# Gate and value products of two token blocks by seven half products instead of eight

## The chip, the cores and the metric

One core of one Trainium2 chip runs the whole program. The metric is device time in microseconds (us). The kernel before took 1024.76 us in the median of three runs (1024.1 to 1025.03). The execution that the profiler recorded took 1026.81 us, of which its trace covers a span of 1025.0 us. Engines are named as in the profile: PE (TensorE), PEld (its weight loads), DVE (VectorE), ACT (ScalarE), POOL (GpSimd), SP (the queue that issues all DMAs here).

## What is computed

A linear attention (random features) is followed by two feed-forward layers on 2304 tokens of 512 features. The change touches the last layer alone:

```python
def _moe2_ref(x, w_gate, w_val, w_out, rms_g):      # x 2304x512, w_gate, w_val 512x1536, w_out 1536x512
    rms = np.sqrt(np.mean(x * x, axis=-1, keepdims=True) + 1e-06)
    xn = x / rms * rms_g
    g = xn @ w_gate
    silu = g * (1.0 / (1.0 + np.exp(-g)))
    val = xn @ w_val
    return (silu * val @ w_out).astype(np.float32)
```

## The kernel before

Tokens are cut into four blocks of 512 columns and a remainder of 256 (`BLK`, index `REM`). The program has two overlapping phases: attention with the first feed-forward layer (`attention`, `moe1`), and then the second layer (`normed`, `moe2`), block by block.

Nothing is ordered by hand. Each piece of work is a node of a `Plan` with an engine (sometimes a choice of engines), an assumed duration, a priority (a position on a common axis; `E1` is the start of the second layer) and buffers out of named pools of slots. `Plan.run` plays the engines forward with these durations, gives each free engine the ready node of the lowest priority whose slots are free, and emits the instructions in that order. On the chip each engine then works through its own list in that fixed order and waits on semaphores. DMAs all go through SP's list.

Every matmul operand is float32 and is cut by `split` into a high part (a CAST on ACT) and a low part (a subtraction, `less`, L389, on DVE or POOL). A product of two such operands takes three matmul passes: high x high, high x low, low x high.

For the second layer, `normed(j)` loads block j's features (`y_d`, four chunks of 128), sums their squares, takes root and reciprocal, scales the chunks, and splits them. `moe2(j)` runs over 12 chunks c of 128 hidden units. `gv(c)` makes gate and value (L991): 4 chunks of features x 3 passes = 12 matmuls each, into a PSUM bank of class `h` (gate) and one of class `t` (value). Silu on ACT (L1002), the product with the value on DVE (L1004) and a split give the operand of `opart(c)` (L1016): for each of 4 groups of 128 tokens 3 matmuls that accumulate over all c in a bank of class `acc`. PSUM has 8 banks: 2 `t`, 2 `h`, 4 `acc`. The weights' 36 units (gate, value and out for each c) are read as 64-bit words, decoded to float32 (`decode`) and split once (`w2_unit`); both parts then stay in SBUF (`wa`, `wb`, some `x`).

## Time and profile before

| | |
|---|---|
| median of 3 runs | 1024.76 us (1024.1 to 1025.03) |
| the profiled execution | 1026.81 us |
| its span in the trace | 1025.0 us |
| PE busy / PEld busy | 1015.3 us (99%) / 864.3 us (84%) |
| DVE / ACT / POOL busy | 519.9 / 470.6 / 85.4 us |
| DMA | 136.86 MB, mean 134 GB/s |
| TensorE clock granted | full speed (2.4 GHz) in every slice |

Busy time of PE counts a matmul from its start to its modelled end; as matmuls overlap, what a matmul costs in a dense row is the distance from start to start, and that is read from the timeline. The second layer starts at 573.5 us and its last matmul ends shortly before 1020 us.

### The profile page before, as it was taken

The numbers are of one execution on the slowest core, as the hardware profiler recorded it, in microseconds if no ns is written. First come the engines' busy times: TensorE is split into PE (matmuls) and PEld (weight loads), VectorE is DVE, ScalarE is ACT, GpSimd is POOL, SyncE is SP. The second block draws the span as 40 slices with busy tenths as digits, with TensorE's granted clock in tenths as the row PEclk, the third lists the DMA queues.
The fourth block names the chain that finished last, engine by engine and source line by source line (L and its number), as shares of the span: only waits on it lengthen the run. The fifth ranks groups of instructions, "written<-read, shape, count | busy, mean of one in ns | idle before, by whom it ended". The sixth has DMA issues, their size and how long they took to land.

```text
span 1025.0 us, 14010 instructions
## 1 busy us (share of the span) xinstructions
PE 1015.3 (99%) x5284; PEld 864.3 (84%) x5284; DVE 519.9 (51%) x1060; ACT 470.6 (46%) x992; POOL 85.4 (8%) x70
## 2 busy tenths in 40 slices
PE   8999999999999999999999999999999999999997
PEld 7888888888888888888889988888888888888897
DVE  5989997744434443278612698822422241213211
ACT  5887897643445434446535566522312231213211
POOL 0111222210101100011100011300000000000000
PEclk9999999999999999999999999999999999999999
DMA  8777888833346322387668343321002100100100
GB/s 250 257 236 255 271 285 299 276 105 110 113 119 196 103 94 83 110 302 263 208 220 273 104 165 124 122 72 42 11 1 73 42 11 1 61 21 1 40 3 21
DMA packets 50644, 136.86 MB, mean 134 GB/s; under 512 B 6160, under 2 KB 7824, under 8 KB 50576
## 3 DMA queue, kind: packets, MB, share of 16 engines
q1 hardware_dynamic: 50576, 135.95, 40.8%
q8 instruction: 42, 0.69, 0.3%
q14 instruction: 26, 0.21, 0.1%
HBM read 114.96 MB, written 20.97 MB: 133 GB/s over the span
## 4 chain that ended last, share of the span: by engine, by line
PE 96%; DMA 2%; ACT 1%; DVE 0%; SPq 0%; issue 0%; ACTq 0%
PE h L840 19%; PE acc L870 19%; PE h L991 14%; PE t L991 14%; PE acc L1016 14%; PE t L726 3%; PE t L599 3%; PE t L596 2%; PE t L666 2%; PE t L721 1%; DMA f<-y 1%; PE acc L596 1%; PE t L768 1%; PE t L669 1%; PE t L730 1%; DMA lt<-in_k_t_dram 0%
## 5 line engine op out<-in xcount | busy, mean ns | idle before, releaser
L389 DVE TENSOR_TENSOR g<-f,g 128x512 fp32r<-128x512 f32 (+1 forms) x135 | 95.8, 709 | 133.6 <-ACT f L510 72.0
L870 PE MATMUL acc<-g,wr 128*128 128x512 f32 (+1 forms) x660 | 151.0, 373 | 0.0
L840 PE MATMUL h<-x,wr 128*128 128x512 f32 x528 | 133.5, 396 | 0.0
L870 PEld LDWEIGHTS acc<-g,wr 128*128 128x128 f32 x660 | 113.7, 189 | 20.0 <-DVE g L389 0.2
L1004 DVE TENSOR_TENSOR f<-t,f 128x512 f32<-128x512 f32 (+1 forms) x58 | 37.1, 640 | 181.7 <-PE t L991 180.9
L840 PEld LDWEIGHTS h<-x,wr 128*128 128x128 f32 x528 | 97.2, 188 | 19.6
L398 ACT CAST g<-f 128x512 fp32r<-128x512 f32 (+1 forms) x60 | 34.9, 582 | 133.9 <-DVE f L1004 87.7
L1002 ACT ACTIVATE f<-h 128x512 f32<-128x512 f32 (+1 forms) x58 | 32.5, 560 | 132.7 <-PE h L991 132.6
L991 PE MATMUL h<-x,wb 128*128 128x512 f32 (+1 forms) x420 | 92.0, 368 | 0.0
L991 PE MATMUL t<-x,wb 128*128 128x512 f32 (+1 forms) x420 | 91.9, 368 | 0.0
L854 ACT ACTIVATE f<-h 128x512 f32<-128x512 f32 (+1 forms) x80 | 44.8, 560 | 102.0 <-PE h L840 95.1
L1016 PE MATMUL acc<-wb,g 128*128 128x512 f32 x378 | 91.6, 389 | 0.0
L991 PEld LDWEIGHTS h<-x,wb 128*128 128x128 f32 x420 | 74.0, 188 | 13.7
L991 PEld LDWEIGHTS t<-x,wb 128*128 128x128 f32 x420 | 73.6, 189 | 13.1
L1016 PEld LDWEIGHTS acc<-wb,g 128*128 128x128 f32 x378 | 70.5, 188 | 14.3
L870 PE MATMUL acc<-g,wu 128*128 128x512 f32 (+1 forms) x300 | 69.6, 375 | 1.2 <-DVE g L389 1.0
L623 ACT ACTIVATE p<-t,sm 128x128 f32<-128x128 f32 x216 | 59.8, 382 | 21.8 <-DVE sm L614 21.8
L991 PE MATMUL h<-x,wa 128*128 128x512 f32 (+1 forms) x300 | 65.8, 368 | 0.0
L991 PE MATMUL t<-x,wa 128*128 128x512 f32 (+1 forms) x300 | 65.7, 368 | 0.0
L840 PE MATMUL h<-x,wu 128*128 128x512 f32 x240 | 61.7, 398 | 0.0
L991 PEld LDWEIGHTS h<-x,wa 128*128 128x128 f32 x300 | 52.8, 188 | 9.7
L991 PEld LDWEIGHTS t<-x,wa 128*128 128x128 f32 x300 | 52.6, 189 | 9.4
(189 smaller groups left out, 1524.4 us busy)
## 6 DMA issues: line engine op xcount, KB each, us to landing
wr<-w1d SPq DMA_DIRECT2D x88, 512.0 KB, 3.5
st<-in_w_out_dram SPq DMA_DIRECT2D x28, 512.0 KB, 4.1
w1d<-wr SPq DMA_DIRECT2D x22, 512.0 KB, 4.1
st<-in_w_in_dram SPq DMA_DIRECT2D x16, 512.0 KB, 4.8
st<-in_w_gate_dram SPq DMA_DIRECT2D x12, 512.0 KB, 4.2
st<-in_w_val_dram SPq DMA_DIRECT2D x12, 512.0 KB, 4.1
f<-y SPq DMA_DIRECT2D x20, 256.0 KB, 4.2
v<-in_v_r_dram SPq DMA_DIRECT2D x16, 260.0 KB, 3.1
```

The source lines that it names most:

```text
L389: return lambda: en.tensor_tensor(out=lo(), in0=src(), in1=f32(hi()), op=ALU.subtract)
L398: first = plan.add("ACT", act(n), prio, lambda: nc.scalar.copy(out=hi(), in_=src()), rd, [whi], after, pre=[blo] if blo is not bhi else [])
L596: nc.tensor.matmul(o, lhsT=xs[0].ap[:, c], rhs=flat(bd), start=True, stop=True)
L599: nc.tensor.matmul(o, lhsT=xs[x].ap[:, cidx, :], rhs=flat(w), start=n == 0, stop=n == 2)
L623: nc.scalar.activation(out=pbuf.ap[:, j0 + i, :], in_=fp.ap[:, i, :], func=AF.Exp, bias=mx.ap[:, i:i + 1])
L840: nc.tensor.matmul(hb.ap[:, :n], lhsT=u.ap[:, wl, kk * P:(kk + 1) * P], rhs=xcols(j, xl, kk)(), start=(gi == 0 and ii == 0), stop=(gi == l ...
L854: lambda: nc.scalar.activation(out=rb.ap[:, :n], in_=hb.ap[:, :n], func=AF.Relu), [hb], [rb])
L870: nc.tensor.matmul(accs[e].ap[:, :n], lhsT=u.ap[:, w, es], rhs=x.ap[:, :n], start=(c == 0 and i == 0), stop=(c == C1 - 1 and i == 2))
L991: nc.tensor.matmul(hb.ap[:, :n], lhsT=w[wl].ap[:, kk * P:(kk + 1) * P], rhs=xn[j, xl, kk].ap[:, :n], start=(i == 0 and kk == 0), stop=(i = ...
L1002: lambda: nc.scalar.activation(out=sb.ap[:, :n], in_=gb.ap[:, :n], func=AF.Silu), [gb], [sb])
L1004: lambda: nc.vector.tensor_tensor(out=sb.ap[:, :n], in0=vb.ap[:, :n], in1=sb.ap[:, :n], op=ALU.mult),
L1016: nc.tensor.matmul(accs[t].ap, lhsT=x.ap[:, cs], rhs=w[wl].ap, start=(c == 0 and i == 0), stop=(c == C2 - 1 and i == 2))
```

## The change

Two blocks of 512 tokens, j and j+1, are worked on together, and two chunks of hidden units, c and c+6. The weights' 256 x 512 block of these chunks (rows: hidden units, columns: features) is seen as a 2 x 2 matrix of A11, A12 (chunk c, first and second half of the features), A21, A22 (chunk c+6); the features as B11, B21 (block j, halves of the features) and B12, B22 (block j+1). The four results then need seven products of halves in place of eight:

- sums of weights: S1 = A21 + A22, S2 = S1 - A11, S3 = A11 - A21, S4 = A12 - S2 (units `g1`, `g2`, `s4` and so on);
- sums of features: T1 = B12 - B11, T3 = B22 - B12, T2 = B22 - T1, T4 = B21 - T2;
- products A11 B11, A12 B21, S2 T2, S3 T3, S1 T1, A22 T4, S4 B22, each 2 chunks x 3 passes = 6 matmuls of 512 columns.

The products run in three PSUM banks a, b, d (`seven`): a bank is read by ACT or DVE in the middle, and the next product accumulates on top of it. One ACT copy and five DVE additions (L1101) with SBUF operands of class `cc` make the four results.

Further: the decoded weights and their sums are made during the first layer, on DVE or POOL (`make_units`, six rounds at priorities 20 to 40), stored to DRAM as float32 (`w2_d`, 9 tiles of 128 x 512 for each c) and read back for each pair of blocks into a ring of 8 slots `wq`, where they are split anew (`read_unit`). The rows of the result no longer accumulate over c in PSUM: each group of 128 tokens gets a bank for c and c+6 (6 matmuls, L1142), which is copied (first round) or added by DVE to an SBUF tile `oa` (L1150). The remainder of 256 tokens runs along with the second pair, with eight products of halves as before. The order of blocks becomes (0, 1), then (2, 3, remainder). The classes `h` and `acc` serve as banks of the products, `t` and `h` as those of the result rows.

```diff
-        "wa": 28, "wb": 42,
+        "xa": 12, "wq": 8, "xb": 4, "xq": 12, "ub": 12, "oa": 10, "cc": 10,
...
+    def make_halves(c, ki, pos):
+        kind, w = (("g", w_gate), ("v", w_val))[ki]
+        gates = last[-2:]
+        ra = raw_unit(pos, (w, c), gates)
+        rb = raw_unit(pos, (w, c + NC2), gates)
...
+        store(pos, (c, kind + "0"), ra)
+        both_sbuf(pos, lambda: t.ap[:, hi_], lambda: ra.ap[:, lo_], lambda: rb.ap[:, lo_], ALU.subtract, 256,
+                  [ra, rb], [(t, 1)])
...
+    def read_unit(c, nm, pos, gates):
+        u = Buf(["wq"])
+        dma(pos, lambda: f32(u.ap[:, 1, :]), lambda: w2_d[c, nm], 262144, r=[b_w2d[c, nm], b_w2a], w=[u], after=gates)
+        split(pos, lambda: f32(u.ap[:, 1, :]), lambda: u.ap[:, 0, :], lambda: u.ap[:, 1, :], 512, [(u, 1)], (u, 0), (u, 1),
+              "ANY")
+        return u
...
+    def operands(j, rv, p0, cls, gates, room):
+        for kk in range(2):
...
+            b11 = scaled(p, j, kk, rv[0], gates, room)
+            b12 = scaled(p, j + 1, kk, rv[1], gates, room)
+            t = Buf(room, view=fview)
+            minus(p, t, b12, b11, 512)
+            two("B11", b11, p)
...
+            minus(p + 0.1, t, b21, t, 512)
+            gates = [plan.nodes[-1]]
...
+    def seven(prio, kind, us, ops, after):
+        a, b, d = Buf(BANKS), Buf(BANKS), Buf(BANKS)
...
+        product(prio, a, ALL, w0, 0, ops["B11"], True, True, [b, d], after)
+        plan.add("ACT", act(512), prio, lambda: nc.scalar.copy(out=s.ap, in_=a.ap), [a, b_w2b], [s], pre=[u2, u3])
+        product(prio, b, ALL, w2_, 0, ops["T2"], True)
+        plus(b, s, u2)
+        product(prio, a, ALL, w0, 256, ops["B21"], False, again=True)
+        product(prio, b, ALL, w2_, 256, ops["T3"], False, again=True)
+        plus(b, s, u3)
+        product(prio, d, ALL, w1_, 0, ops["T1"], True)
+        plus(d, u3, u3)
+        product(prio, b, ALL, w1_, 256, ops["T4"], False, again=True)
+        plus(b, s, s)
+        nd = product(prio, d, ALL, us["s4"], 256 * k4, ops["B22"], False, again=True)
+        plus(d, u2, u2)
...
+    def out_rows(prio, j, t, us, parts, oa, first, last):
+        o = Buf(["t", "h"])
...
+        if first:
+            copy(prio, lambda: oa.ap, lambda: o.ap, 512, [o, b_w2b], [oa])
+        else:
+            plan.add("DVE", dve(512), prio,
+                     lambda: nc.vector.tensor_tensor(out=oa.ap, in0=o.ap, in1=oa.ap, op=ALU.add), [o, oa], [oa])
...
-    for j in range(B + 1):
-        normed(j, [gv_nodes[2] if j else h_nodes[5]])
-        moe2(j)
+    sets = [read_units(c, E1 + (c - 1.0 if c else -7.0), []) for c in range(NC2)]
+    hidden0 = moe2(0, sets, x01, None)
...
+    x23 = operands(2, rv23, G0[0] + NC2 - 0.5, ["x", "xa"], hidden0[3:4], room)
+    sets = [read_units(c, G0[1] + c - 1.0, hidden0[4:5]) for c in range(NC2)]
+    moe2(1, sets, x23, xr2)
```

The lists of three engines show the new order; names are tile class and number, a row reads engine line, operation, out<-in, shape. First PE, before, in a later block of the second layer, from the end of a value product to the result rows:

```order
L991 MATMUL t_7267<-x_6611,wb_6418 128x512
L991 MATMUL t_7267<-x_6653,wb_6418 128x512
L991 MATMUL t_7267<-x_6664,wb_6418 128x512
L991 MATMUL t_7267<-x_6714,wb_6418 128x512
L1016 MATMUL acc_6921<-wb_6354,g_7237 128x512
L1016 MATMUL acc_6921<-wb_6355,g_7237 128x512
L1016 MATMUL acc_6921<-wb_6354,g_7238 128x512
```

PE in the second pair (fifth round, c = 4): the end of S2 T2 + S3 T3 in bank h_9200, the value's A11 B11 in h_9252, then A22 T4 again in h_9200:

```order
L1081 MATMUL h_9200<-x_7774,wq_9146 128x512
L1081 MATMUL h_9200<-xa_8008,wq_9146 128x512
L1081 MATMUL h_9252<-x_7735,wq_9188 128x512
L1081 MATMUL h_9252<-x_7960,wq_9188 128x512
L1081 MATMUL h_9252<-x_7736,wq_9188 128x512
L1081 MATMUL h_9252<-x_7961,wq_9188 128x512
L1081 MATMUL h_9252<-x_7735,wq_9188 128x512
L1081 MATMUL h_9252<-x_7960,wq_9188 128x512
L1081 MATMUL h_9200<-x_7837,wq_9154 128x512
```

A bank that before was written by one dense group is now written, read by DVE and written again, with one product of 6 matmuls of another bank in between.

DVE, before, in a later block: products of value and silu (L1004), low parts (L389) and copies of finished rows:

```order
L1004 TENSOR_TENSOR f_8021<-t_8016,f_8021 128x512
L389 TENSOR_TENSOR g_8043<-f_8021,g_8042 128x512
L1004 TENSOR_TENSOR f_8070<-t_8065,f_8070 128x512
L1033 COPY f_8087<-acc_7529 128x512
L389 TENSOR_TENSOR g_8090<-f_8070,g_8089 128x512
L1033 COPY f_8102<-acc_7541 128x512
```

DVE, after, where PE passes from the first pair to the second (result rows L1150, new operands L1020, L928, L394, the first weight unit wq_7793, the first addition of the second pair L1101):

```order
L928 TENSOR_TENSOR xb_7972<-xb_7864,xb_7972 128x512
L1150 TENSOR_TENSOR oa_6822<-t_7952,oa_6822 128x512
L1150 TENSOR_TENSOR oa_6834<-h_7964,oa_6834 128x512
L394 TENSOR_TENSOR xa_8039<-xb_7972,xa_8038 128x512
L1150 TENSOR_TENSOR oa_6848<-h_7978,oa_6848 128x512
L1150 TENSOR_TENSOR oa_6863<-t_8030,oa_6863 128x512
L1150 TENSOR_TENSOR oa_6882<-t_8042,oa_6882 128x512
L394 TENSOR_TENSOR wq_7793<-wq_7793 128x512
L1150 TENSOR_TENSOR oa_6903<-h_8053,oa_6903 128x512
L1101 TENSOR_TENSOR cc_8004<-acc_7993,cc_8003 128x512
```

DVE's list now holds additions that free PE's banks, new operands and weight units in one row.

SP, before, in the last part of the first layer (remainder): feature loads of block 0 stand among the weight loads.

```order
DMA wr_5604<-w1d_116 128x1024
DMA f_5626<-y_89 128x512
DMA f_5635<-y_89 128x512
DMA wr_5648<-w1d_118 128x1024
DMA wr_5669<-w1d_117 128x1024
```

SP, after, at the same place: the second half of the first pair's features comes behind the last weight load.

```order
DMA wr_6155<-w1d_123 128x1024
DMA wr_6195<-w1d_125 128x1024
DMA st_6324<-y_89 128x512
DMA st_6334<-y_90 128x512
DMA st_6347<-y_90 128x512
DMA dw_6356<-y_89 128x512
```

The feature loads for the first products of the second layer moved behind the whole weight traffic of the first.

## Rows read from the trace of the kernel before

**Rows 1.** The page, part 1: busy us (share of the span) xinstructions.

```profile
PE 1015.3 (99%) x5284; PEld 864.3 (84%) x5284; DVE 519.9 (51%) x1060; ACT 470.6 (46%) x992; POOL 85.4 (8%) x70
```

**Rows 2.** The page, part 4: chain that ended last, by engine, by line.

```profile
PE 96%; DMA 2%; ACT 1%; DVE 0%; SPq 0%; issue 0%; ACTq 0%
PE h L840 19%; PE acc L870 19%; PE h L991 14%; PE t L991 14%; PE acc L1016 14%; PE t L726 3%; PE t L599 3%; PE t L596 2%; PE t L666 2%; PE t L721 1%; DMA f<-y 1%; PE acc L596 1%; PE t L768 1%; PE t L669 1%; PE t L730 1%; DMA lt<-in_k_t_dram 0%
```

**Rows 3.** Waits of PE: line waited for, us in total, times, longest.

```profile
PE h L596 <- DMA lt<-in_k_t_dram: 1.2, 1, 1.2
...
PE acc L870 <- DVE g L389: 1.0, 2, 0.5
```

**Rows 4.** Windows: us, busy (x) of PE, PEld, DVE, ACT, POOL; PEclk, DMA, GB/s.

```profile
200.00:425.00 225.00, 225.00 (x1271) 193.25 (x1270) 95.70 (x238) 100.39 (x258) 17.06 (x13) 1.00 0.37 117
425.00:525.00 100.00, 100.00 (x460) 83.10 (x459) 64.51 (x111) 49.96 (x84) 9.97 (x7) 1.00 0.66 227
525.00:573.50 48.50, 47.33 (x376) 45.95 (x375) 17.89 (x28) 25.92 (x59) 0.74 (x1) 1.00 0.74 238
573.50:671.00 97.50, 97.50 (x438) 80.94 (x438) 79.14 (x120) 56.79 (x88) 21.77 (x15) 1.00 0.40 130
671.00:769.50 98.50, 98.50 (x436) 81.56 (x435) 29.23 (x40) 24.20 (x38) 0.00 (x0) 1.00 0.12 33
966.00:1019.80 53.80, 53.75 (x371) 49.82 (x370) 12.18 (x27) 10.65 (x27) 0.00 (x0) 1.00 0.06 21
```

**Rows 5.** PE's timeline, second layer: start us, us, line op, xcount.

```profile
703.35 2.88 PE L991 MATMUL h<-x,wa 128*128 128x512 f32 x12
706.07 2.88 PE L991 MATMUL t<-x,wa 128*128 128x512 f32 x12
708.79 2.88 PE L1016 MATMUL acc<-wa,g 128*128 128x512 f32 x12
```

**Rows 6.** PE's timeline, matmuls of 256 columns.

```profile
544.31 1.60 PE L870 MATMUL acc<-g,wr 128*128 128x256 f32 x12
545.75 1.60 PE L840 MATMUL h<-xr,wu 128*128 128x256 f32 x12
```

**Rows 7.** DVE's timeline where it is full.

```profile
625.37 0.69 DVE L389 TENSOR_TENSOR wb<-st,wb 128x512 fp32r<-128x512 f32 x1 [0.36 <-ACT wb L398]
625.98 0.42 DVE L438 TENSOR_SCALAR st<-st 128x512 f32<-128x512 f32 x1
626.43 0.69 DVE L441 SCALAR_TENSOR_TENSOR st<-st 128x512 uint32<-128x512 uint32 x1
627.04 0.68 DVE L1004 TENSOR_TENSOR f<-t,f 128x512 f32<-128x512 f32 x1
627.64 0.42 DVE L427 TENSOR_SCALAR st<-st 128x512 uint32<-128x512 uint32 x1
```

**Rows 8.** Timeline of all engines: POOL and DVE at once.

```profile
595.35 1.60 POOL L389 TENSOR_TENSOR wb<-st,wb 128x512 fp32r<-128x512 f32 x1 [2.39 <-ACT wb L398]
...
595.87 1.63 DVE L389 TENSOR_TENSOR g<-f,g 128x512 fp32r<-128x512 f32 x1
```

**Rows 9.** DVE's groups by shape: busy, mean ns, idle before.

```profile
L389 DVE TENSOR_TENSOR g<-f,g 128x512 fp32r<-128x512 f32 x109 | 84.7, 777 | 107.1 <-ACT f L510 60.6 <-ACT g L398 32.8 <-PE t L666 7.8
...
L1004 DVE TENSOR_TENSOR f<-t,f 128x512 f32<-128x512 f32 x47 | 32.5, 691 | 148.8 <-PE t L991 148.0 <-ACT f L1002 0.8
...
L389 DVE TENSOR_TENSOR g<-f,g 128x256 fp32r<-128x256 f32 x26 | 11.0, 424 | 26.4 <-ACT f L510 11.4 <-PE acc L870 10.1 <-ACT g L398 4.7
...
L962 DVE RECIPROCAL st<-st 128x256 f32<-128x256 f32 x1 | 1.8, 1754 | 1.1 <-ACT st L959 1.1
```

**Rows 10.** Timeline of all engines: from the value's last matmul to DVE.

```profile
673.43 2.88 PE L991 MATMUL t<-x,wa 128*128 128x512 f32 x12
...
676.42 0.69 DVE L1004 TENSOR_TENSOR f<-t,f 128x512 f32<-128x512 f32 x1 [5.18 <-PE t L991]
```

**Rows 11.** The page, part 6: DMA, count, KB each, median us to landing.

```profile
f<-y SPq DMA_DIRECT2D x20, 256.0 KB, 4.2
```

**Rows 12.** The chain in order of time: start us, us, what.

```profile
542.03 6.54 DMA f<-y
```

310 lines of the change are left out of this document (198 added, 112 removed).

## The prediction

> **What bounds the kernel now.** I read the page's busy line first: PE 1015.3 us of a span of 1025.0, DVE half, POOL little [rows 1]. Busy time of PE is no proof, so the second view is the chain of work that ended last: 96% of it is PE, and the three matmul lines of the second layer (L991 gate, L991 value, L1016 out) hold 42% [rows 2]. Third, what PE waited for: after the start only 1.0 us in the whole run, for a low part on DVE [rows 3]. Fourth, a table by stage: from 573.5 us to the last matmul PE has no gap, while DVE is busy 81% of the first block's time and 30% of the next one's [rows 4]. Fifth, the price of a matmul in that dense row: groups of 12 follow each other at 703.35, 706.07, 708.79, so 2.72 us / 12 = 0.2267 us for 512 columns [rows 5]; groups of 12 with 256 columns stand 1.44 us apart, 0.120 us each [rows 6]. So the time falls by what is taken from PE's list, less what PE then has to wait for.
>
> **What it removes.** For two blocks and two chunks, gate and value took 2 x 2 x 24 = 96 matmuls of 512 columns; seven products of 6 matmuls for each kind are 84. Twelve fewer, for 2 pairs of blocks and 6 rounds: 144 x 0.2267 = **32.6 us** off PE's path. The result rows keep their count (2 chunks x 3 passes for each group of tokens), the remainder keeps its 48 of 256 columns a round, and the sums of squares stay. Nothing else leaves PE.
>
> The Trainium skill, "TensorE: Matmul & The Clock Gate", section Back-to-back issue gap, gives about 131 ns for a 512-column matmul in a stream of weight loads and matmuls; by that figure the 144 would bring 18.9 us. No row here shows such a rate.
>
> **What it adds on other engines, and where PE may wait for it.**
>
> *DVE's price.* Where DVE's list is full, operations of 512 float32 elements start 0.61, 0.61 and 0.60 us after each other, though each is recorded as 0.68 to 0.69 long [rows 7]: they overlap, and 0.61 is what one costs in a row. For 256 elements I take the recorded 0.42 less the same 0.08, 0.34; a reciprocal of 256 is 1.75 [rows 9]. Beside a POOL operation of 1.60 us a DVE operation with two SBUF inputs took 1.63 instead of 0.69 [rows 8], 0.94 more; over the run that form averages 0.777, while L1004, with one input in PSUM, stays at 0.691 [rows 9].
>
> *First pair, rounds 1 to 5.* Counted from the lists between the first addition of round 1 and that of the second pair, DVE has 211 operations (195 of 512, 11 of 256, 5 reciprocals): 195 x 0.61 + 11 x 0.34 + 5 x 1.75 = 131.4 us. PE has 688 matmuls of 512 columns between the same points: 156.0 us. DVE is filled to 84%, a shade over the 81% of the stage at 573.5 us where PE stayed dense [rows 4]. POOL has 25 operations there; blocked DVE costs between nothing and 25 x 0.94 = 23.5 us, I take half: 143 of 156 us, 92%. That is fuller than anything in the second layer before, and now PE depends on DVE in the middle of each product group, not only at its end. A wait costs nothing so long as another product lies between: the last matmul of the value's group starts at 673.43 + 11 x 0.2267 = 675.92, DVE starts at 676.42 and ends 0.69 later at 677.11 [rows 10], 0.96 us after that group's last slot ended at 676.15; one product in between covers 1.36. So 0.40 us are spare; a DVE operation that is just running (0.61) may eat them, a blocked one (1.63) costs up to 1.2. Queued behind a late addition on DVE are the low parts of the next operands and the result rows, which hold PE's banks. With 2 or 3 thin spots in each of the 5 rounds and a blocked operation in some of them I take **+3 us**; the bounds are 0 and 12.
>
> The Trainium skill, "SBUF — State Buffer", section Who interferes with whom, says that DVE operations with two SBUF inputs and POOL's reads lock each other out, and that those with at most one SBUF input don't contend. Rows 8 and 9 show the same split; by it the additions into banks (L1101, L1150, 89 of the 211) are never blocked themselves, only those queued behind a blocked one.
>
> *First layer to second.* PE has 28.3 us of work between the root sums of blocks 0 and 1 and the first product (4 matmuls of 512 and 228 of 256). Against it stands a chain: two roots on ACT (about 2.5), four reciprocals (7.0), 13 operations of 512 and two of 256 on the first half of the features (8.6), then loads of the second half, which are gated by a subtraction of the first half and stand behind the last weight load on SP, 4.2 us to landing [rows 11] (6.54 in the worst case seen [rows 12]), and four operations (2.4): 24.7, with SP's issue and the hops between engines some 27 us. It fits, barely; S2 T2, two products later, needs seven more operations (4.3 us) in 2.7 us. **+1 us**, bounds 0 and 5.
>
> *First pair to second.* The second pair's operands take the first pair's slots, so their last half is made while PE works off result rows. From the last addition of the first pair to the first of the second DVE has 32 operations, 19.5 us, and POOL about 8, which at half price block 3.8: 23.3. PE has 16 groups of six, 96 x 0.2267 = 21.8 us, before it needs what follows. **+1.5 us**, bounds 0 and 5.
>
> *Second pair.* 215 operations of 512 on DVE, 131 us, against 882 x 0.2267 + 288 x 0.120 = 234.5 us on PE: 56%, five POOL operations. **+0.6 us**, bounds 0 and 4.
>
> *First layer.* Decoding moves from 425 to 671 us into the stretch from about 200 us on, with 48 small sums more, and 60 stores on SP. In those two stages DVE did some 70 us more than at its level outside them, of which about 25 are splits that now follow the reads; 45 + 48 x 0.34 = 61 us go into 225 us where it was busy 95.7, so 43% becomes 70%. The stages with 65% and 81% kept PE dense [rows 4], which is why I take only **+0.5 us**; bounds -1 (the wait of 1.0 us [rows 3] may go) and +6. DMA share there was 0.37 [rows 4], and has room for 19 MB of weights and 14 MB of stores.
>
> *Reads of the weights.* 108 reads of 256 KB with a split each replace 36 splits; DVE's part is in the counts above, ACT gains 72 casts in about 400 us. The ring of 8 slots must be ahead of PE; taken as covered (rival C).
>
> *The end.* The last row was copied and stored, now it is added and stored: 0.
>
> **Sum.** -32.6 + 3 + 1 + 1.5 + 0.6 + 0.5 = -26.0 us. The profiled execution of 1026.81 becomes 1000.8; it lay 2.05 above the median of 1024.76, so the median becomes **998.8, predicted 999**.
>
> **Rivals.**
>
> A. DVE becomes the bound of the first pair. For it: 92% with the lock, and dependencies both ways. Against it: 81% cost nothing [rows 4]. Price: all 25 blocks at 0.94 give 155 us of DVE; if a tenth of the stage is still idle through dependencies, 172 us stand against PE's 156: +16 instead of +3, **1012**.
>
> B. The first layer pays for the weight sums: operations that wait for a DMA stand in front of the low parts that PE needs. A wait of 0.5 us as the two seen (1.0 us in two [rows 3]), at 18 of the 36 units, is 9 us: **1007**.
>
> C. The slower side: the ring runs dry. Two of the 8 slots hold the out weights of the round before, so seven units go through six slots, and the last can be read only when the first product's unit is free. From there to its use lie about nine products, 12 us; the way is 4.2 to land [rows 11], a cast and a low part, 5.5 to 6.5 us. If landing took 6.54 [rows 12] and the low part queued behind a full DVE, PE would wait each round. Beyond 26.0 / 12 = 2.2 us a round over 12 rounds the kernel is slower than before; at 4 us a round it is 999 + 48 = **1047**. The second pair's DVE at 56% and an idle DMA (0.12 [rows 4]) speak against it.
>
> D. It doesn't bring what the count says: the matmuls removed cost less than 0.2267 each. At the 0.120 us of the cheapest matmul in the rows [rows 6] it would be 144 x 0.120 = 17.3 us off, **1014**. Against it, every dense row of 512 columns costs 0.2267. By the figure of the Trainium skill's page on TensorE named above it would be 1013.
>
> **How the numbers follow.** Forecast 0.64, A 0.18, B 0.10, C 0.04, D 0.02, and 0.02 for something that ends within 0.2% of before; 0.2% is about what a measurement of this kernel can tell from no change. The lowest bound is 1024.76 - 32.6 - 1 = 991. Upward the terms' bounds add to more than is likely at once; B and most of A are inside 1011, C and D outside. Range 991 to 1011. Faster 0.94, same 0.02, slower 0.04.
>
> **What would show it.** The page should count 144 fewer matmuls and PE some 990 us. The timeline should show groups of six at 1.36 us. Waits of PE should name DVE's additions (L1101, L1150) first, a few us in all, nearly all of it before the second pair; the span's first 525 us should end where they did. Wrong would be: long waits for the low parts of `wq` (C), DVE over 90% with PE gaps throughout the first pair (A), or the first product of the second layer more than 5 us later than 573.5.

## The result, and the profile after

| | before | after |
|---|---|---|
| median | 1024.89 us (1024.1 to 1025.35, 4 runs) | 1006.5 us (1005.34 to 1007.82, 4 runs) |
| ratio | | 0.9822, 95% interval 0.9805 to 0.9839 |
| profiled execution | 1026.81 us | 1006.28 us |
| span in the trace | 1025.0 us | 1004.5 us |

The change is worth 18.4 us in the medians and 20.5 us between the two profiled executions. The forecast was 999 us with a range of 991 to 1011: the direction and the range held, and 7.5 us of the expected gain are missing.

The page's busy line and the first line of the chain, after:

```profile
PE 989.2 (98%) x5140; PEld 838.4 (83%) x5140; DVE 712.2 (71%) x1374; ACT 525.6 (52%) x1097; POOL 122.3 (12%) x101
PE 88%; DVE 4%; DMA 4%; issue 1%; ACT 1%; POOL 1%; SPq 0%; ACTq 0%; POOLq 0%; DVEq 0%
```

Against [rows 1] PE has 144 instructions fewer (5140 for 5284), and DVE is busy for 712 us in place of 520. Against [rows 2] DVE now holds 4% of the chain, where it had 0%. The price of a matmul is the same as in [rows 5]; PE's timeline of after (start us, us, line, count) at the end of the passage from the first pair to the second:

```profile
767.33 1.52 PE L1142 MATMUL h<-wq,ub 128*128 128x512 f32 x6
768.69 1.52 PE L1142 MATMUL t<-wq,ub 128*128 128x512 f32 x6
770.05 1.52 PE L1081 MATMUL acc<-xa,wq 128*128 128x512 f32 x6
```

Groups of six stand 1.36 us apart, 0.2267 us a matmul. So the removal itself brought 144 x 0.2267 = 32.6 us, the profiled execution should have become 1026.81 - 32.6 = 994.2 us, and 1006.28 - 994.2 = **12.1 us** were lost again. The prediction allowed 6.6 for that.

**Where the 12.1 us are.** PE's waits, after (line waited for: us in total, times, longest):

```profile
PE acc L1081 <- ACT xa L403: 3.1, 1, 3.1
PE acc L1081 <- DVE f L894: 1.8, 1, 1.8
...
PE t L1142 <- DVE oa L1150: 0.7, 4, 0.2
PE h L1081 <- DVE xa L394: 0.4, 1, 0.4
```

In the kernel before PE waited 1.0 us for DVE after its start, in the whole run [rows 3]. The two long waits are one event each, and the windows by stage (us, busy of PE, PEld, DVE, ACT, POOL, granted clock, DMA share, GB/s) show where:

```profile
573.50:595.00 21.50, 18.85 (x84) 14.90 (x83) 16.08 (x28) 12.80 (x23) 0.00 (x0) 0.92 0.33 91
595.00:750.00 155.00, 155.00 (x685) 128.07 (x684) 135.19 (x200) 84.78 (x147) 29.92 (x23) 1.00 0.39 113
750.00:770.00 20.00, 16.88 (x66) 12.88 (x65) 18.66 (x24) 5.87 (x10) 8.23 (x5) 0.91 0.27 96
770.00:990.00 220.00, 219.31 (x1098) 186.17 (x1098) 140.06 (x207) 74.86 (x128) 6.80 (x5) 1.00 0.22 62
```

In the long stage between 595 and 750 us PE is dense beside a DVE that is busy 87% of the time. The losses sit where the first layer passes into the second, and where the first pair passes into the second; and in both the clock granted falls below 1.00. PE's timeline at the first of them:

```profile
576.40 1.55 PE L1081 MATMUL h<-x,wq 128*128 128x512 f32 x6
...
583.27 2.75 PE L1081 MATMUL acc<-x,wq 128*128 128x512 f32 x7 [1.84 <-DVE f L894]
585.82 0.63 PE L1081 MATMUL acc<-xa,wq 128*128 128x512 f32 x1
586.24 0.63 PE L1081 MATMUL acc<-x,wq 128*128 128x512 f32 x1
```

The first product starts with no wait of its own. At 581.04 comes the last matmul before a wait; the next one starts at 583.27, 2.01 us later than in a dense row. The first three matmuls behind it start 0.23 to 0.34 us after each other, the next eight 0.39 to 0.43 us in place of 0.23 (585.82 to 586.24): 512 columns in 0.427 us are the lower level of the clock, 1.2 GHz. The clock granted did not fall while PE waited, but 0.7 us after it had started again:

```profile
583.30:584.00 0.70, 0.70 (x3) 0.61 (x4) 0.70 (x2) 0.34 (x1) 0.00 (x0) 1.00 0.00 0
584.10:587.10 3.00, 3.00 (x9) 2.32 (x8) 1.34 (x3) 2.11 (x4) 0.00 (x0) 0.50 0.30 90
```

Taken from start to start the place costs 0.8 (a short wait for a low part before it) + 2.0 + 1.7 for the matmuls behind the wait, most of it the eight slow ones = **4.5 us**. The long wait is not for an operand. It is for a PSUM bank that still holds finished features of the first layer's remainder, and the copy that frees it (L894) stands in DVE's list behind the operands of the second layer:

```profile
581.60 0.69 DVE L928 TENSOR_TENSOR dw<-dw,dw 128x512 f32<-128x512 f32 x1
582.20 0.69 DVE L394 TENSOR_TENSOR xa<-dw,xa 128x512 fp32r<-128x512 f32 x1
582.80 0.75 DVE L894 COPY f<-acc 128x256 f32<-128x256 f32 x2
```

At the second place, between the pairs:

```profile
751.07 2.88 PE L1142 MATMUL t<-wq,ub 128*128 128x512 f32 x12
753.79 2.88 PE L1142 MATMUL h<-wq,ub 128*128 128x512 f32 x12
756.51 1.93 PE L1081 MATMUL acc<-x,wq 128*128 128x512 f32 x7
761.56 0.79 PE L1081 MATMUL acc<-xa,wq 128*128 128x512 f32 x1 [3.12 <-ACT xa L403]
762.15 0.63 PE L1081 MATMUL acc<-x,wq 128*128 128x512 f32 x1
```

This wait is for an operand: 3.3 us from start to start, and seven matmuls 0.37 to 0.63 us apart behind it (1.9 us), **5.4 us** with the remainders. PE could not have gone on with the result rows that follow in its list either. The four groups of six from 751.07 on fill the two banks of class `t` and the two of class `h`, and DVE's additions, which free them, stand behind the operands in its list; between these two lines no addition starts:

```profile
751.27 0.69 DVE L1150 TENSOR_TENSOR oa<-h,oa 128x512 f32<-128x512 f32 x1
...
762.65 0.68 DVE L1150 TENSOR_TENSOR oa<-t,oa 128x512 f32<-128x512 f32 x1
```

In the second pair four more waits cost 0.45 us each from start to start, 1.8 us, and in the first pair 0.25. Together these are 12.0 us. Besides, the first product starts 1.0 us later than the matmuls moved ahead of it explain (576.40 for 573.55, with 1.9 us of matmuls moved), and from PE's last matmul to the end the span is 0.6 us shorter; so the places add up to 12.4 us, 0.3 more than the 12.1. The 1.0 us is not shown to come from the change: with the same list up to there the first product starts at 575.36 in the run e_prio2 and at 573.16 in e_late, both described below. Of the 3.2 us between e_late and this kernel 2.6 are there by PE's 300th matmul (49.3 and 51.9 us): at the start of the span equal matmuls stand 0.43 us apart, up to 9.0 us in the one and 14.0 in the other, and 0.22 after that. (The kernel before shows the same up to 13.5 us, though its page gives full clock for the first slice.)

**Why DVE is late there.** DVE and POOL, after, beside each other at the second place:

```profile
754.63 1.62 DVE L394 TENSOR_TENSOR x<-st,x 128x512 fp32r<-128x512 f32 x1
756.18 1.78 DVE L928 TENSOR_TENSOR st<-st,st 128x512 f32<-128x512 f32 x1
759.12 1.74 DVE L928 TENSOR_TENSOR xb<-st,xb 128x512 f32<-128x512 f32 x1 [1.16 <-POOL x L394]
```
```profile
753.35 2.35 POOL L394 TENSOR_TENSOR x<-st,x 128x512 fp32r<-128x512 f32 x1 [3.79 <-ACT x L403]
755.66 1.74 POOL L394 TENSOR_TENSOR wq<-wq 128x512 fp32r<-128x512 f32 x1
757.37 1.72 POOL L394 TENSOR_TENSOR x<-xb,x 128x512 fp32r<-128x512 f32 x1
759.04 1.26 POOL L394 TENSOR_TENSOR wq<-wq 128x512 fp32r<-128x512 f32 x1
```

Three DVE operations with both inputs in SBUF take 1.62 to 1.78 us in place of 0.69, each while POOL works, as in [rows 8], and before the third DVE stands idle 1.16 us for a low part that POOL makes. At the first place the same is seen: from 556.9 to 567.5 us ten DVE operations on the first half of the features take 10.6 us beside POOL, where 0.61 each would be 6.1. My theory (T) after this reading: the losses are two passages, where DVE's list, slowed by POOL, frees PE's banks or makes its operands too late, plus the clock's answer to PE's idle time. The rivals: the sums of weights (B), loads behind the weight traffic (L), and a cost of the new staging itself, apart from the seven products.

### The profile page after: what moved, and what is told of

It reads as the page before. It is cut to its first block, busy times and chain, and to the rows that moved or that the text cites. A ratio compares the mean times of both kernels' runs of the same rounds, so it can differ in the third digit from the quotient of the medians.

```text
span 1004.5 us, 14617 instructions
## 1 busy us (share of the span) xinstructions
PE 989.2 (98%) x5140; PEld 838.4 (83%) x5140; DVE 712.2 (71%) x1374; ACT 525.6 (52%) x1097; POOL 122.3 (12%) x101
## 4 chain that ended last, share of the span: by engine, by line
PE 88%; DVE 4%; DMA 4%; issue 1%; ACT 1%; POOL 1%; SPq 0%; ACTq 0%; POOLq 0%; DVEq 0%
PE acc L875 18%; PE h L845 18%; PE acc L1081 11%; PE t L1142 11%; PE h L1081 10%; PE t L1081 3%; PE t L731 3%; PE t L604 2%; PE t L601 2%; PE t L671 2%; DMA st<-y 2%; PE t L726 1%; PE h L1142 1%; DVE cc L1101 1%; DVE wq L394 1%
## 5 line engine op out<-in xcount | busy, mean ns | idle before, releaser
L1142 PE MATMUL t<-wq,ub 128*128 128x512 f32 x462 | 114.5, 392 | 0.7 <-DVE oa L1150 0.7
L1081 PE MATMUL acc<-x,wq 128*128 128x512 f32 x321 | 111.5, 396 | 1.8 <-DVE f L894 1.8
L403 ACT CAST wq<-wq 128x512 fp32r<-128x512 f32 x108 | 66.3, 619 | 87.3 <-DMA wq<-w2d4g 14.8
L1142 PEld LDWEIGHTS t<-wq,ub 128*128 128x128 f32 x462 | 86.7, 189 | 20.6 <-DVE oa L1150 2.4
L394 DVE TENSOR_TENSOR g<-f,g 128x512 fp32r<-128x512 f32 (+1 forms) x67 | 46.4, 693 | 70.1 <-ACT f L515 58.8
L1081 PE MATMUL acc<-xa,wq 128*128 128x512 f32 x231 | 89.9, 396 | 3.1 <-ACT xa L403 3.1
L394 DVE TENSOR_TENSOR wq<-wq 128x512 fp32r<-128x512 f32 x99 | 74.1, 756 | 25.5 <-ACT wq L403 25.0
L1081 PE MATMUL h<-x,wq 128*128 128x512 f32 x255 | 81.0, 390 | 0.0
L1081 PEld LDWEIGHTS acc<-x,wq 128*128 128x128 f32 x321 | 61.1, 191 | 15.1 <-DVE f L894 2.3
L1081 PE MATMUL h<-xa,wq 128*128 128x512 f32 x201 | 69.3, 390 | 0.4 <-DVE xa L394 0.4
L628 ACT ACTIVATE p<-t,sm 128x128 f32<-128x128 f32 x216 | 60.0, 383 | 18.1 <-DVE sm L619 18.1
L1101 DVE TENSOR_TENSOR cc<-acc,cc 128x512 f32<-128x512 f32 x84 | 57.7, 686 | 14.8 <-PE acc L1081 13.8
L1150 DVE TENSOR_TENSOR oa<-t,oa 128x512 f32<-128x512 f32 x75 | 50.8, 686 | 23.1 <-PE t L1142 22.7
L441 ACT ACTIVATE dw<-st 128x512 f32<-128x512 f32 x68 | 46.6, 696 | 22.8 <-DMA st<-in_w_out_dram 9.4
```

Source lines behind the costliest of these rows:

```text
L394: return lambda: en.tensor_tensor(out=lo(), in0=src(), in1=f32(hi()), op=ALU.subtract)
L403: first = plan.add("ACT", act(n), prio, lambda: nc.scalar.copy(out=hi(), in_=src()), rd, [whi], after, pre=[blo] if blo is not bhi else [])
L441: lambda: nc.scalar.activation(out=out(), in_=hf(), func=AF.Abs, scale=65536.0), [(st, 1)], [w])
L628: nc.scalar.activation(out=pbuf.ap[:, j0 + i, :], in_=fp.ap[:, i, :], func=AF.Exp, bias=mx.ap[:, i:i + 1])
L1081: nc.tensor.matmul(bank.ap[:, cols], lhsT=u.ap[:, wl, c0 + kk * P:c0 + (kk + 1) * P], rhs=x[kk][xl].ap[:, :cols.stop - cols.start], start= ...
L1101: lambda: nc.vector.tensor_tensor(out=out.ap, in0=bank.ap, in1=x.ap, op=ALU.add), [bank, x], [out])
```

## The experiments

Unless said otherwise the edits are to the changed kernel, and "ratio" is to the kernel before on the same chip, with its 95% interval.

**e_early: the first pair's operands sooner.**

```diff
-    rv01 = [rms(j, E1 - 10.0, [h3[4 + 2 * j]], ["xa"], room, ["wq"]) for j in range(2)]
-    x01 = operands(0, rv01, E1 - 8.0, ["x", "xa"], [h3[9]], room)
+    rv01 = [rms(j, E1 - 14.0, [h3[4 + 2 * j]], ["xa"], room, ["wq"]) for j in range(2)]
+    x01 = operands(0, rv01, E1 - 12.0, ["x", "xa"], [h3[9]], room)
```

> The first pair's roots and operands get a priority 4 chunks of the first layer earlier; PE then has 40.9 us of work (by the instruction list, at 0.2267 and 0.120 us) between the root sums and the first product, in place of 28.3. Theory T: in the changed kernel PE loses about 4.4 us near 581 us, because the operands are made too late on a full DVE, and because the clock falls to its lower level for some nine matmuls after that wait. Then the wait and the slow matmuls are gone here, and the median is some 4 us lower, about 1002 to 1003. Rival L (the loads of the second half are what is late, behind the weight loads on SP): they move up by the same 12.6 us, so the wait would go as well, but DVE's scaling would be seen to wait for a DMA. Rival B (the first layer is slowed by the weight sums on DVE): the earlier operands take DVE's time at a fuller place, PE waits in the first layer before 570 us, and the time stays at 1006 or rises.

1001.46 us (1000.21 to 1002.42), ratio 0.9767 [0.9751, 0.9783]: 5.0 us less. No wait and no slow matmul is left there behind the first product (ahead of it stand 1.1 us for a low part of the first layer that POOL made); the window reads, with the clock at 1.00,

```profile
573.50:595.00 21.50, 21.50 (x103) 18.06 (x102) 12.88 (x22) 9.74 (x16) 0.62 (x1) 1.00 0.32 97
```

The second place is as it was (3.3 us). So the first loss was DVE's lateness. Rival L would give the same time here; against it stand that in the changed kernel DVE took up the second half's features with no idle time before them, and that e_nopool below takes the loss away without an earlier priority for any load.

**e_prio2: all of the second pair's operands half a round sooner.**

```diff
-    x23 = operands(2, rv23, G0[0] + NC2 - 0.5, ["x", "xa"], hidden0[3:4], room)
+    x23 = operands(2, rv23, G0[0] + NC2 - 1.0, ["x", "xa"], hidden0[3:4], room)
```

> The second pair's operands get a priority half a round earlier, so that DVE's list has their second half ahead of the last result rows of the first pair rather than behind them. Theory T: PE's wait of 3.3 us near 758 us for an operand and the slow matmuls behind it (5.3 us in all) come from that order in DVE's list; the wait should shrink to 0 to 2 us, the half-speed matmuls vanish, and the median fall to 1001 to 1004. Rival X (DVE has simply too much to do there, whatever the order): the wait goes over to the result rows' banks, PE loses the same 5 us at other lines, and the median stays at 1005 to 1008.

1009.78 us (1008.08 to 1014.17), ratio 0.9855 [0.9834, 0.9875], slower than the changed kernel. My expectation was wrong, and rival X's 1005 to 1008 was missed as well. PE's list now has four products of the second pair ahead of twelve groups of result rows, and PE waits in three of them and then for the rows (the clock granted from 750 to 770 us is 0.74):

```profile
PE t L1142 <- DVE oa L1150: 2.4, 5, 1.7
PE acc L1081 <- DVE xa L394: 2.0, 1, 2.0
...
PE acc L1081 <- ACT xa L403: 1.7, 1, 1.7
PE acc L1081 <- DVE x L394: 1.1, 1, 1.1
```

An earlier priority makes nothing sooner on a full engine; it puts work in front of other work, and since the order is fixed ahead from assumed durations, it also pulls products forward on PE that then stand before their operands have been made.

**e_nopool: nothing for POOL from the second layer's preparation on.**

```diff
-         plan.add("DVE", Shared(dve(n)), prio, tt(nc.vector), rd, wr, alts=[("POOL", pool(n), tt(nc.gpsimd))])
+         plan.add("DVE", Shared(dve(n)), prio, tt(nc.vector), rd, wr,
+                  alts=[("POOL", pool(n), tt(nc.gpsimd))] if prio < E1 - 20 else [])
```
(and "DVE" for "ANY" in the splits of operands, weight units and hidden units)

> In the second layer's preparation and in the layer itself nothing is given to POOL: all low parts and sums of operands go to DVE (27 operations more on DVE). Theory T with the lock: near 558 and near 754 us DVE operations of two SBUF inputs took 1.2 to 1.8 us beside POOL's in place of 0.69; alone, DVE is done with the two pieces of work together as fast as both engines were, so both waits of PE (about 4.4 and 5.3 us) shrink, by a third to all of it: 998 to 1004. If POOL's share is a real help (no lock), DVE has 27 x 0.61 = 16 us more to do, of which about 5 us fall on each of the two places: the waits grow, 1008 to 1014.

999.5 us (998.3 to 1000.09), ratio 0.9747 [0.9733, 0.9761]: 7.0 us less, though DVE has more to do. The low parts of the weights from 549 us on, by shape (count | busy us, mean ns), first the changed kernel, then this one:

```profile
L394 DVE TENSOR_TENSOR wq<-wq 128x512 fp32r<-128x512 f32 x93 | 70.1, 761 | 25.1 <-ACT wq L403 24.6
```
```profile
L394 DVE TENSOR_TENSOR wq<-wq 128x512 fp32r<-128x512 f32 x102 | 69.0, 685 | 26.1 <-ACT wq L403 25.6
```

DVE does 102 of them in less time than 93: what POOL took over, DVE lost by waiting. The edit also takes away DVE's waits for what POOL makes, as the 1.16 us above; in the 7.0 us the two are not told apart. The first place has no long wait any more, the four of 0.34 us in the second pair are gone, and one is left between the pairs, of 3.5 us:

```profile
754.84 4.33 PE L1143 MATMUL t<-wq,ub 128*128 128x512 f32 x12 [3.37 <-ACT xa L403]
```
```profile
754.00 1.29 DVE L1151 TENSOR_TENSOR oa<-t,oa 128x512 f32<-128x512 f32 x2
```

The profile names a cast on ACT, which ended at that moment. These matmuls read `wq` and `ub` and don't need it; they need a bank of class `t`, which the first of DVE's two row additions frees at 754.69, and these stand behind the operands in DVE's list. The Trainium skill, "SBUF — State Buffer", section Who interferes with whom, says that a DVE operation with two SBUF inputs and POOL's reads of SBUF exclude each other, while one with at most one SBUF input doesn't contend outside the modes that use both ports. The two lines agree with the first half; by it POOL's help on such data is worth something only while DVE is idle or busy with operations of the second kind.

**e_late: the second pair's last operands behind the result rows** (POOL as in the changed kernel).

```diff
+            p += kk * late
             two("T3", b12, p + 0.1)
             two("B22", b22, p + 0.1)
...
-    x23 = operands(2, rv23, G0[0] + NC2 - 0.5, ["x", "xa"], hidden0[3:4], room)
+    x23 = operands(2, rv23, G0[0] + NC2 - 0.5, ["x", "xa"], hidden0[3:4], room, 1.5)
```

> The four later operands of the second half (T3, B22, B21, T4) of the second pair get a priority 1.5 rounds later, so that in DVE's list they stand behind the result rows of the first pair's last round; POOL is used as in the changed kernel. The products need them 1.36 to 9.5 us after the first one. Theory O: PE's wait at the change of pairs (5.3 us with the slow matmuls) is a matter of order: DVE spends its time there on operands that are needed last, ahead of work that frees PE's banks or makes the first operand. Then the wait falls to 0 to 2 us, the slow matmuls vanish, and the median is 1001 to 1004. Rival W (DVE has more work between the pairs than PE has, whatever the order): the wait moves into the first products of the second pair, T3 or T1 late in place of B11, and the median stays at 1005 to 1008.

1001.09 us (996.51 to 1003.22), ratio 0.9747 [0.9723, 0.9771], as theory O expected; of the five executions the profiled one was the fastest (996.51). PE's list shows what changed: in the changed kernel the value's products B11 and T2 of the second pair stand ahead of the last four groups of result rows, and it is T2 that waits; here one of these groups stands ahead of B11, and the other three, the remainder's 12 matmuls of 256 columns and the gate's B11 come between it and the first T2. DVE's list changed with it: its row additions at 750.05, 753.46 and 755.14 us stand among the operands and free banks. The place, PE's timeline:

```profile
752.85 1.07 PE L1082 MATMUL acc<-x,wq 128*128 128x512 f32 x4
754.72 0.73 PE L1082 MATMUL acc<-x,wq 128*128 128x512 f32 x2 [0.81 <-POOL wq L394]
755.30 1.53 PE L1143 MATMUL t<-wq,ub 128*128 128x512 f32 x6
```

One wait of 0.8 us is left, for a low part on POOL, and no slow matmul. In the changed kernel 24 matmuls, 5.4 us, had stood behind the wait; DVE had finished their operands by 748.4 us (its last low part of a hidden unit), but the first bank for them came free only with the addition at 762.65. The edit mended both orders at once. At the first place this execution still has the wait of 2.0 us, without slow matmuls behind it.

**e_np_late: both.** The diffs of e_nopool and e_late together.

> Both edits at once: no POOL from the second layer's preparation on, and the later operands of the second pair behind the result rows. Without POOL the median was 999.5, of which a wait of 3.5 us near 751 us and seven matmuls of 0.43 us in place of 0.23 (1.4 us), 4.9 us in all, were left at the change of pairs. Theory O: they vanish, 994.5 to 996. Rival W: DVE's work there is too much in any order, and the median stays at 998 to 1001.

995.09 us (992.31 to 995.42), ratio 0.969 [0.9675, 0.9706]: faster than both kernels, 11.4 us under the changed one. After 574 us PE's longest loss from start to start is 0.75 us, and where the pairs meet the window has PE full (compare the 16.88 of after):

```profile
750.00:770.00 20.00, 20.00 (x93) 16.63 (x92) 18.36 (x31) 6.78 (x13) 0.00 (x0) 1.00 0.41 144
```

**e_np_join: four result additions fewer between the pairs**, in the place of the later operands.

```diff
+                both = g == 0 and j in JOIN and c >= NC2 - 2
+                if both and c == NC2 - 2:
+                    joined.append(u)
+                    continue
                 for t in range(NB // P):
-                    out_rows(p, j0 + j, t, unit_sets[c], [(u[0, j], t * P), (u[1, j], t * P)],
+                    parts = [(v[dc, j], t * P) for v in joined + [u] for dc in range(2)] if both else [
+                        (u[0, j], t * P), (u[1, j], t * P)]
+                    out_rows(p, j0 + j, t, [unit_sets[c - 1], unit_sets[c]] if both else [unit_sets[c]], parts,
```
(with JOIN = (0,), block 0 of the pair)

> No POOL as above, and the result rows of block 0 (4 groups of 128 tokens) of the first pair's last two rounds are summed in one PSUM bank (12 matmuls) in place of two: four additions of DVE fewer, 4 x 0.61 = 2.4 us, between the pairs; operands in the order of the changed kernel. Rival W (too much DVE work at the change of pairs): the wait of 3.5 us there shrinks by about 2.4 us and the slow matmuls with it, 995.5 to 997.5. Theory O (order alone): the additions that PE waits for still stand behind the operands, so the wait stays near 3.5 us or moves, 998.5 to 1001.

997.63 us (996.73 to 998.43), ratio 0.9721 [0.9708, 0.9734]. The wait of 3.5 us shrank to 0.9 with no slow matmul, which is what rival W had said for this edit; the time lies 0.1 us above its range and below theory O's. Both readings of the second place are thus true in part: DVE has about as much work there as PE, so 2.4 us less of it takes most of the loss away, and so does a better order; the better order gave more (995.09).

**e_nosums: the weight sums left out.**

```diff
         store(pos, (c, kind + "0"), ra)
-        both_sbuf(pos, lambda: t.ap[:, hi_], lambda: ra.ap[:, lo_], lambda: rb.ap[:, lo_], ALU.subtract, 256,
-                  [ra, rb], [(t, 1)])
...
-        store(pos, (c, kind + "2"), t)
...
+        store(pos, (c, kind + "1"), rb)
+        store(pos, (c, kind + "2"), ra)
+        store(pos, (c, "s4"), rb, slice(256 * ki, 256 * ki + 256))
```

> The changed kernel without the sums of weights in the first layer: the plain weights are stored in place of S1 to S4 (the output is not the reference's), as many stores, reads, splits and matmuls. 48 operations of 256 columns on DVE or POOL are left out, 48 x 0.34 = 16 us of DVE between about 200 and 425 us. Rival B (the first layer pays for the sums): the first layer ends 1.3 us or more earlier, 1002 to 1005, or lower if the later waits go with it. Theory T: the sums lie beside PE's work and the waits at the two transitions have nothing to do with them: 1005.5 to 1007.5, with both waits where they were.

1008.66 us (1007.61 to 1010.15), ratio 0.9825 [0.9812, 0.9839], against 0.9822 for the changed kernel: nothing gained, and both waits where they were (2.0 and 3.3 us from start to start). Rival B falls as far as the sums go; the decoding, which stays in the first layer here, is in e_eight below. The time is a little above the expected 1005.5 to 1007.5. In the profiled execution, the slowest of the five (1010.15), 3.5 us of it lie in the first layer: at 311 us PE waits 1.7 us for an activation on ACT (L628), and soon after it eight matmuls stand 0.38 to 0.43 us apart; at the second place thirteen matmuls are slow in place of seven. Whether the missing sums have to do with that wait no run shows.

**e_eight: eight products for seven.** With the seven products the units S2, one for gate and one for value, and S4 go too: six units a round are read and split in place of nine. The diff shows the products alone.

```diff
-            for i, kind in enumerate("gv"):
-                r[kind], nd = seven(p + 0.3 * i, kind, us, ops, [h_nodes[C1 - 1]])
+            for i, (dc, j) in enumerate(((0, 0), (0, 1), (1, 0), (1, 1))):
+                for kind in "gv":
+                    bank = Buf(BANKS)
+                    for hh in range(2):
+                        nd = product(p + 0.1 * i, bank, ALL, us[f"{kind}{dc}"], 256 * hh, ops[f"B{hh + 1}{j + 1}"],
+                                     hh == 0, hh == 1, after=[h_nodes[C1 - 1]])
```

> Seven products are undone alone: eight products of halves per kind, each result summed in its PSUM bank, with no sums of features and none of results; pairing of blocks, units kept in DRAM and read again, result rows and the first layer's work (sums of weights too) stay. The second row of results is computed with the sum of weights in place of the plain weights, so its output is not the reference's; the work is the same. PE has 144 matmuls more, 5284 as before. If the 144 matmuls cost 0.2267 us each and the additions between banks cost nothing, the time is 1006.5 + 32.6 = 1039. Theory T: the missing operand sums (T1 to T4, 24 operations of DVE or POOL for each pair) and result additions unload DVE at the two transitions, some 5 to 10 us of waits go, 1029 to 1034, so that the reorganisation without the seven products costs 4 to 9 us against the kernel before. If the two waits stem from the pairing, the late loads or the clock alone and not from the sums, they stay, and the time is 1037 to 1040.

1029.29 us (1027.79 to 1031.44), ratio 1.004 [1.0026, 1.0055]. PE is back at 5284 matmuls, and the time is 22.8 us above the changed kernel, not 32.6. It has one wait of its own: for a bank that the silu reads, whose tile lies in a pool that opens only when the first layer's is closed (the silu starts at 590.22, after a table load of 1.28 us on ACT). Matmuls at the lower clock follow:

```profile
588.18 0.51 PE L875 MATMUL acc<-g,wr 128*128 128x256 f32 x3
590.87 5.30 PE L1067 MATMUL h<-x,wq 128*128 128x512 f32 x15 [2.17 <-ACT cc L1109]
```

2.3 + 0.3 + 7 x 0.2 = 4 us from start to start, and no wait between the pairs. Without that it would stand at 1025, where the kernel before stands: pairing of blocks, six of the nine units read again and result rows added in SBUF cost nothing that shows, and the decoding and the sums of weights in the first layer, which it still makes, don't either. What the seven products lose comes from their own additions and sums of features and from the three more units a round; these two are not told apart.

**e_warm, e_warm2: PE kept busy where it waited.** Matmuls whose result is overwritten.

```diff
+            for _ in range(more):
+                nc.tensor.matmul(bank.ap[:, cols], lhsT=u.ap[:, 0, c0:c0 + P], rhs=x[0][0].ap, start=True, stop=True)
...
-        product(prio, a, ALL, w0, 0, ops["B11"], True, True, [b, d], after)
+        product(prio, a, ALL, w0, 0, ops["B11"], True, True, [b, d], after,
+                more=9 if prio == G0[0] else 0)
...
-        product(prio, b, ALL, w2_, 0, ops["T2"], True)
+        product(prio, b, ALL, w2_, 0, ops["T2"], True, more=15 if prio == G0[1] + 0.3 else 0)
```
(e_warm2; in e_warm the 15 stood at `prio == G0[1]`)

> The changed kernel with matmuls more on PE, whose results are overwritten: 9 ahead of the first product of the first pair (9 x 0.2267 = 2.0 us, the length of PE's wait for a bank a few products later) and 15 ahead of T2's second half in the second pair (3.4 us, the wait for an operand). The operands arrive when they did, so PE is busy in place of idle, and nothing else is sooner. Theory K: the nine and the eight matmuls at 0.43 us in place of 0.23 behind the two waits are the granted clock's answer to the idle time alone; they vanish and the time falls by their excess, 1.8 + 1.8 us, to 1002.5 to 1004. If the clock fell for another reason (a load on the chip at that place), the slow matmuls stay, and the time is 1006 to 1008.

> As the run before with more matmuls, but the 15 now stand where PE waits in the second pair: ahead of T2 of the value, whose second half of operands is late. (In that run they stood ahead of T2 of the gate, behind the wait, and cost their own 3.4 us: 1007.9 = 1006.5 + 3.4 less about 2 at the first place.) Theory K: idle time alone brings the clock down. PE is busy at both places, no matmul behind them starts 0.43 us after the one before, and the time falls by some 1.7 us at each place: 1002.5 to 1004. If the clock falls there for another reason, the slow matmuls stay: 1005.5 to 1007.

e_warm: 1007.94 us (1007.16 to 1010.63), ratio 0.9832 [0.9817, 0.9847]. I had put the 15 at the gate's T2; the one that waits is the value's. The second place was as before, and the 3.4 us came on top. e_warm2: 1004.22 us (1001.73 to 1006.01), ratio 0.979 [0.9771, 0.9809], 2.3 us less than the changed kernel with 24 matmuls more. That is just above the expected 1002.5 to 1004, and the intervals of the two ratios overlap slightly, so the trace is the stronger evidence. The second place:

```profile
756.08 3.56 PE L1080 MATMUL acc<-x,wq 128*128 128x512 f32 x15
759.48 0.39 PE L1083 MATMUL acc<-x,wq 128*128 128x512 f32 x1
759.71 0.46 PE L1083 MATMUL acc<-xa,wq 128*128 128x512 f32 x1
...
760.88 0.50 PE L1083 MATMUL acc<-xa,wq 128*128 128x512 f32 x1 [0.48 <-DVE xa L394]
761.22 0.39 PE L1083 MATMUL acc<-x,wq 128*128 128x512 f32 x1
```

The operand comes when it came, but what follows runs at 0.23 us, and the clock granted from 573.5 to 595 and from 750 to 770 us is 1.00 in place of 0.92 and 0.91. So at the second place PE's idle time is what brought the clock down. At the first place this run alone doesn't show it, since e_prio2 and e_late had the same wait of 2.0 us there and no slow matmul behind it. The gain stays under the 3.3 us of the slow matmuls; other short waits came up (0.6 and 0.65 us in the first pair).

**e_early_late: both passages mended, POOL kept.** The diffs of e_early and e_late together.

> POOL as in the changed kernel; the first pair's roots and operands 4 chunks earlier, and the later operands of the second pair behind the result rows. Alone the two brought 5.0 us (1001.5) and between 5.4 us (1001.1 as the median, which held executions with and without the slow matmuls at the first place) and 9.8 (996.5, without). Theory: the two places are all that is lost in the changed kernel apart from the four waits of 0.45 us in the second pair, so the median is 995.5 to 997.5. If POOL's lock costs more than these places (in the first pair too), it stays above 998.

998.63 us (997.54 to 999.67), ratio 0.9736 [0.9723, 0.975], 1 us above the expectation: beside the two passages POOL costs some 3 us more (995.09 without it). They are in the trace: 0.97 us at 755, 0.73 at 622, and 0.34 four times in the second pair (0.45 with the matmul behind each). One of these four in the changed kernel, DVE's list and POOL's:

```profile
849.80 1.78 DVE L394 TENSOR_TENSOR wq<-wq 128x512 fp32r<-128x512 f32 x1
...
853.31 1.27 DVE L1150 TENSOR_TENSOR oa<-t,oa 128x512 f32<-128x512 f32 x2
```
```profile
849.66 1.37 POOL L394 TENSOR_TENSOR ub<-cc,ub 128x512 fp32r<-128x512 f32 x1 [37.05 <-ACT ub L403]
```

A blocked low part at 849.80 pushes the row addition at 853.31 back, for whose bank PE waits. POOL has five such operations in the second pair, and PE waits like this behind four of them.

**e_np_late2: e_np_late with the first pair's operands two chunks sooner.**

```diff
-    rv01 = [rms(j, E1 - 10.0, [h3[4 + 2 * j]], ["xa"], room, ["wq"]) for j in range(2)]
-    x01 = operands(0, rv01, E1 - 8.0, ["x", "xa"], [h3[9]], room)
+    rv01 = [rms(j, E1 - 12.0, [h3[4 + 2 * j]], ["xa"], room, ["wq"]) for j in range(2)]
+    x01 = operands(0, rv01, E1 - 10.0, ["x", "xa"], [h3[9]], room)
```

> No POOL from the second layer's preparation on, later operands of the second pair behind the result rows, and the first pair's roots and operands 2 chunks of the first layer earlier. Without the last edit the median was 995.1, and PE had no wait over 0.8 us from 574 us on; by the theory nothing is left to gain there: 994 to 996. If an unseen part of the first layer's last stretch still bears on it, 992 to 994.

995.69 us (995.32 to 998.72), ratio 0.971 [0.9696, 0.9723]: no further gain, as expected. The bound is 1024.9 - 32.6 = 992.3 us, and e_np_late is within 3 us of it.

## Why the prediction was right, and where it missed

| step of the prediction | predicted | in the profile of after |
|---|---|---|
| 144 matmuls at 0.2267 | -32.6 | -32.6: 5140 matmuls, 1.36 us for six |
| first pair, rounds 1 to 5 | +3 (0 to 12) | +0.25 |
| first layer to second | +1 (0 to 5) | +4.5 |
| first pair to second | +1.5 (0 to 5) | +5.4 |
| second pair | +0.6 (0 to 4) | +1.8 |
| first layer | +0.5 (-1 to 6) | +1.0, not shown to be the change's |
| the end | 0 | -0.6 |
| sum | -26.0 | -20.2 by these rows, -20.5 measured |

- **The removal** came out as predicted: its price was taken from a dense row, and the places that lost a matmul are such rows. Rival D is out. The 131 ns of the Trainium skill, "TensorE: Matmul & The Clock Gate", section Back-to-back issue gap, is not the price here: the rows of after show 0.2267 us as those of before did.
- **The first pair** was the term I feared, and it cost nothing. DVE was busy 135 of 155 us, 87%, with POOL at 30 us beside it, and still one product between a bank's writing and its next use was cover enough. The additions into banks were not slowed beside POOL, as the prediction said (686 ns on average for L1101 and for L1150). Rival A had the mechanism right (the lock) but the wrong place: blocked operations hurt where no dense row of other products stands behind them.
- **First layer to second.** The chain of roots, operands and loads was counted to fit barely, and it did: the first product starts with no wait, and the operands of S2 T2, for which the +1 stood, cost 0.8. Two things were left out. The lock had no price here, though beside POOL the ten operations named above took 10.6 us for 6.1. And the same DVE list holds the copies of the remainder's finished features, which free banks that the second layer now uses. Which banks the products take was told by the change (`h` and `acc`); who frees them was not followed up. e_early and e_nopool, each by another way, take the whole loss away.
- **First pair to second.** The sum set 23.3 us of DVE against 21.8 us of PE, "16 groups of six before it needs what follows". It compared two totals, and the order inside them decides. Sixteen is the count of the row groups, but in PE's list two of them stand before the last products and four behind the T2 that waits: ten groups, B11 and one matmul are 67 x 0.2267 = 15.2 us. The four could not have run sooner either, since the additions that free their banks stood behind the operands in DVE's list. That is the step that failed; e_late, where both orders are mended, loses only 1.1 us there. DVE's total was too small as well: 25.7 us passed between the two additions (743.80 to 769.50) for 23.3. Half price for the lock was too little at this place: three operations in a row paid 0.9 to 1.1 us each.
- **The clock** had no term at all. Of the 9.9 us at the two passages some 3.3 are matmuls at 1.2 GHz behind a wait (1.6 and 1.7); e_warm2 shows for the second place that they follow from the idle time. That the range held all the same is luck: its upper end was there for A and B, neither of which happened, and costs that it had not counted filled that room.
- **The second pair** was mis-sized by 1.2 us; the mechanism is the one named for the first pair (a blocked operation ahead of a row addition).
- **The first layer** and rival B: e_nosums and e_eight show no cost of the sums of weights, and e_eight none of the decoding. **The ring of weights** (C) never ran dry: in the changed kernel no wait of PE names `wq`, and in e_late and e_early_late one of 0.8 us does, for a low part on POOL.
- **The signs.** "Waits of PE should name DVE's additions (L1101, L1150) first" did not come: L1101 is not among them and L1150 has 0.7 us, in the second pair; first stand an operand's cast (3.1 us) and the copy L894 (1.8). The count of matmuls, PE's 989 us and the groups at 1.36 us did come, and the first product is 2.9 us later than before, inside the 5 that were allowed.

## What to carry to other kernels

Look at the passages between stages first: a stage in its steady run hides a busy engine that the passage doesn't, and a dependency there can be a bank's or a slot's release rather than an operand. When two engines' totals are set against each other, follow the order inside them too: here 5.4 us of matmuls stood behind a wait of 3.3, their operands long made, but their banks held by additions that stood behind operands in DVE's list. Moving the least urgent operands back mended both. Don't count an engine as help if it shares what its neighbour needs: giving POOL's operations back to a DVE that was 87% busy made the kernel 7 us faster.

## What the runs showed of the hardware

- After a wait on a PE that had been dense, 512-column matmuls could start 0.43 us apart (clock granted 0.50, 1.2 GHz) for some five to thirteen of them, then 0.23 again. After the waits of 3.3 to 3.5 us it came in every profile that had one (the changed kernel, e_early, e_nopool, e_nosums, e_warm). After the wait of 2.0 us at the first place it came in the changed kernel and in e_nosums, and not in e_prio2 and e_late, whose gaps there were the same to 0.01 us. It also came after a loss of 1.9 us (e_nosums at 311 us) and of 2.3 us (e_eight). In the changed kernel the clock fell 0.7 us after PE had started again. What tells these apart no run here shows.
- POOL's low parts beside a full DVE bought nothing: 93 DVE operations with POOL's help took 70.1 us, 102 without it 69.0 us.
